# Attention on one core: K, Q and V loaded and outputs stored in groups of heads, waits folded into instructions

## Chip, cores, metric

One core of one Trainium2 chip. The metric is the device time of one execution in microseconds (us), from runs without a profile; the profile comes from a run of its own.

## The reference, cut to what matters

```python
B, H, Sq, Sk, D = 16, 32, 192, 1024, 128          # bfloat16
scores = jnp.einsum("bhqd,bhkd->bhqk", q, k) * D ** -0.5
p = softmax(scores, axis=-1)
out = jnp.einsum("bhqk,bhkd->bhqd", p, v)
```

There are 512 independent heads. Of each, the kernel reads 256 KB of K, 256 KB of V and 48 KB of Q, and writes 48 KB.

## The kernel before

All heads run through one software pipeline. A head has three units of 64 queries. A schedule of "virtual times" (one step is one unit) fixes each engine's order of instructions; semaphores do the rest. For each unit: QK on TensorE (8 matmuls), the maximum over key chunks on VectorE (`mx`), the maximum over partitions on GpSimd (`ar`), a bias matmul that subtracts it (`bi`), the exponential on ScalarE (`ex`). For each head: VectorE copies V beside a column of ones (`build_v`), TensorE multiplies P with it (`pv`), VectorE takes the reciprocal of the row sums (`rc`), ScalarE scales (`nm`), and the result is stored.

```python
NBK, NBQ, NBVR, NBV, NBO = 4, 3, 3, 2, 3      # slots: K, Q (4 heads each), V, V with ones, output
vt_lk = lambda h: NU * h - PFK * NU           # place of the K load in the order, PFK = 3 heads ahead
vt_lv = lambda h: vt_vc(h) - PFV * NU         # V: PFV = 2 heads ahead of its copy

def load_k(e, h=h, ks=ks):
    ins = e.dma_start_transpose(kT[:, ks], kf[h].rearrange("(kk c) d -> kk (c d)", c=NCH))
    if h >= NBK:
        ins.wait_op(s_qk, NU * (h - NBK + 1), "sem-ge")     # slot free
    ins.then_inc(s_k[ks], 16)

def load_v(e, h=h, vrs=vrs):
    ins = e.dma_start(vraw[:, vrs], vf[h].rearrange("(kk c) d -> kk c d", c=NCH))
    ...                                                     # same queue (SyncE) as K and Q

def build_v(e, h=h, vrs=vrs, vs=vs):
    if h >= NBV:
        e.wait_ge(s_pv, h - NBV + 1)                        # a wait of its own
    e.tensor_copy(v1[:, vs, :, 0:D], vraw[:, vrs]).wait_op(s_v[vrs], ...).then_inc(s_vc, 1)

def qk(e, ...):
    if j == 0:
        e.wait_ge(s_k[ks], 16 * (h // NBK + 1))             # a wait of its own
    ...
add("pe", vt_qk(u), qk)      # vt: u
add("dve", vt_mx(u), mx)     #     u + 1
add("pool", vt_ar(u), ar)    #     u + 2
add("pe", vt_bi(u), bi)      #     u + 3.4: after the QK of unit u + 3
```

## Time and profile before

| | us |
|---|---|
| median of 4 runs at first, of 16 in the end | 1340.7, 1342.2 |
| span of the profiled run | 1336.7 |
| TensorE's floor: 512 heads of 2.295 | 1175 |
| VectorE waiting for V | 131.0 |
| lost on TensorE before bias matmuls | 147 |

The last line is worked out from the trace: a bias matmul starts 29 ns after the last QK matmul if nothing is missing; what goes beyond is lost time of TensorE. (The page's idle time shows less of it, since the modelled ends of matmuls reach 160 ns over the next start.) The lines that carry this are in the prediction.

One more view: the loading queue (SyncE's) in order of time. Columns: start, length of the issue in us, queue, line, what.

```profile
646.02 1.17 SPq L153 DMA_TRANSPOSE qT<-in_q_dram  x1
647.24 1.31 SPq L146 DMA_TRANSPOSE kT<-in_k_dram  x1
648.59 0.58 SPq L160 DMA_DIRECT2D vraw<-in_v_dram  x1
649.21 1.24 SPq L146 DMA_TRANSPOSE kT<-in_k_dram  x1
650.50 0.74 SPq L160 DMA_DIRECT2D vraw<-in_v_dram  x1
651.28 1.46 SPq L146 DMA_TRANSPOSE kT<-in_k_dram  x1
652.79 0.57 SPq L160 DMA_DIRECT2D vraw<-in_v_dram  x1
653.40 1.34 SPq L146 DMA_TRANSPOSE kT<-in_k_dram  x1
654.79 0.57 SPq L160 DMA_DIRECT2D vraw<-in_v_dram  x1
```

Each issue starts 0.04 us after the last has ended. The queue is never idle: all its pauses over 0.1 us sum to 6 us of 1324.

### The profile page before, as it was taken

The numbers are of one execution on the slowest core, as the hardware profiler recorded it, in microseconds if no ns is written. First come the engines' busy times: TensorE is split into PE (matmuls) and PEld (weight loads), VectorE is DVE, ScalarE is ACT, GpSimd is POOL, SyncE is SP. The second block draws the span as 40 slices with busy tenths as digits, with TensorE's granted clock in tenths as the row PEclk, the third lists the DMA queues.
The fourth block names the chain that finished last, engine by engine and source line by source line (L and its number), as shares of the span: only waits on it lengthen the run. The fifth ranks groups of instructions, "written<-read, shape, count | busy, mean of one in ns | idle before, by whom it ended". The sixth has DMA issues, their size and how long they took to land.

```text
span 1336.7 us, 54938 instructions
## 1 busy us (share of the span) xinstructions
PE 1243.3 (93%) x22016; PEld 1049.0 (78%) x22016; DVE 1175.9 (88%) x2563; ACT 1115.3 (83%) x2561; POOL 861.3 (64%) x1540
## 2 busy tenths in 40 slices
PE   7999999999999999999999999999999999999997
PEld 6777788778887787878878787777887777877776
DVE  7888898899889898989888898888888898988886
ACT  6888888888888888888888888888888888888887
POOL 5666666666666666666666666666666666666665
PEclk9999999999999999999999999999999999999999
DMA  9999999999999999999999999999999999999998
GB/s 209 239 248 241 246 250 240 239 251 240 252 241 251 241 258 233 252 240 258 243 243 243 240 248 246 233 236 248 240 241 247 232 254 240 251 245 246 234 235 174
DMA packets 774397, 322.43 MB, mean 241 GB/s; under 512 B 659456, under 2 KB 708608, under 8 KB 774144
## 3 DMA queue, kind: packets, MB, share of 16 engines
q1 hardware_dynamic: 716800, 293.72, 107.9%
q10 hardware_dynamic: 57344, 25.20, 9.3%
q8 instruction: 176, 2.88, 0.9%
q14 instruction: 77, 0.63, 0.2%
HBM read 134.22 MB, written 25.17 MB: 119 GB/s over the span
## 4 chain that ended last, share of the span: by engine, by line
DMA 45%; PE 35%; DVE 9%; SPq 5%; POOL 4%; issue 2%; ACT 0%
DMA vraw<-in_v_dram 45%; PE ps L243 13%; PE ps L214 12%; PE ps L197 10%; DVE rmx L206 5%; SPq L146 5%; POOL hi L209 4%; DVE v L176 4%; DVE rinv L254 0%; SPq L153 0%; ACT osb L261 0%; ACT pT L222 0%
## 5 line engine op out<-in xcount | busy, mean ns | idle before, releaser
L209 POOL PARTITION_ALL_REDUCE hi<-rmx x1536 | 861.1, 561 | 469.8 <-DVE rmx L206 412.7
L206 DVE TENSOR_REDUCE rmx<-ps 128x64 bf16<-128x512 f32 x1536 | 986.1, 681 | 19.9 <-PE ps L197 6.9
L222 ACT ACTIVATE pT<-ps 128x512 bf16<-128x512 f32 x1536 | 853.8, 592 | 91.1 <-PE ps L214 57.7
L214 PE MATMUL ps<-hi,negsel 128*128 128x512 bf16 x1536 | 588.9, 383 | 84.6 <-POOL hi L209 81.3
L197 PEld LDWEIGHTS ps<-qT,kT 128*128 128x128 bf16 x12288 | 517.7, 98 | 128.0 <-issue 6.9
L197 PE MATMUL ps<-qT,kT 128*128 128x64 bf16 x12288 | 609.4, 193 | 5.9 <-DMA kT<-in_k_dram 5.8
L243 PEld LDWEIGHTS ps<-v,pT 128*96 128x96 bf16 x8192 | 550.2, 124 | 30.1
L243 PE MATMUL ps<-v,pT 128*96 128x129 bf16 x8192 | 568.4, 221 | 0.0
L261 ACT ACTIVATE osb<-ps,rinv 96x128 bf16<-96x128 f32 x1024 | 316.7, 358 | 127.6 <-DVE rinv L254 123.0
L176 DVE COPY v<-vraw 128x1024 bf16<-128x1024 bf16 x512 | 217.2, 424 | 134.7 <-DMA vraw<-in_v_dram 131.0
L214 PEld LDWEIGHTS ps<-hi,negsel 128*128 128x128 bf16 x1536 | 149.4, 97 | 126.5 <-POOL hi L209 104.0
L254 DVE RECIPROCAL rinv<-ps 96x2 f32<-96x2 f32 x512 | 79.4, 155 | 2.7 <-PE ps L243 2.7
L222 ACT ACT_TABLE_LOAD x1 | 1.3, 1283 | 0.7 <-PEq L309 0.7
L132 DVE MEMSET negsel<- 128x64 uint32 x1 | 0.1, 112 | 0.8 <-PEq L309 0.8
L309 POOL MEMSET const-float32-0.0<- 128x1 f32 x1 | 0.1, 98 | 0.2 <-issue 0.2
L133 DVE MEMSET negsel<- 1x128 bf16 x1 | 0.2, 165 | 0.1
L309 POOL MEMSET const-bfloat16-1.0<- 128x1 bf16 x1 | 0.1, 102 | 0.0
L309 POOL MEMSET const-uint8-127<- 128x1 uint8 x1 | 0.1, 101 | 0.0
L309 POOL MEMSET const-float32-1.0<- 128x1 f32 x1 | 0.1, 98 | 0.0
L134 DVE MEMSET v<- 128x16 bf16 x1 | 0.1, 72 | 0.0
## 6 DMA issues: line engine op xcount, KB each, us to landing
vraw<-in_v_dram SPq DMA_DIRECT2D x512, 256.0 KB, 4.4
out_dram<-osb ACTq DMA_DIRECT2D x512, 48.0 KB, 3.7
kT<-in_k_dram SPq DMA_TRANSPOSE x512, 4.9
qT<-in_q_dram SPq DMA_TRANSPOSE x128, 4.9
```

The source lines that it names most:

```text
L133: e.memset(negsel[0:1, :], -1.0).wait_op(s_init, 1, "sem-ge").then_inc(s_init, 1)
L146: ins = e.dma_start_transpose(kT[:, ks], kf[h].rearrange("(kk c) d -> kk (c d)", c=NCH))
L176: e.tensor_copy(v1[:, vs, :, 0:D], vraw[:, vrs]).wait_op(s_v[vrs], 16 * (h // NBVR + 1), "sem-ge").then_inc(s_vc, 1)
L197: ins = e.matmul(ps[:, bank, c * QW:(c + 1) * QW], kT[:, ks, c, :], rhs, start=(c == 0), stop=False, skip_group_check=True)
L206: e.tensor_reduce(rmx[:, rs, :], src, AX.X, ALU.max).wait_op(s_qk, u + 1, "sem-ge").then_inc(s_mx, 1)
L209: e.partition_all_reduce(hi[:, hs, :], rmx[:, rs, :], P, RMAX).wait_op(s_mx, u + 1, "sem-ge").then_inc(s_ar, 1)
L214: e.matmul(dst, negsel[:, :], rhs, start=False, stop=True, skip_group_check=True).wait_op(s_ar, u + 1, "sem-ge").then_inc(s_bi, 1)
L222: e.activation(pT[:, psl, :, q0:q0 + QW], src, ACTF.Exp, scale=scale).wait_op(s_bi, u + 1, "sem-ge").then_inc(s_ex, 1)
L243: ins = e.matmul(ps[0:MT, ob, t * (D + 1):(t + 1) * (D + 1)], lhsT, v1[:, vs, c, :], start=(c == 0), stop=(c == NCH - 1), skip_group_check ...
L254: e.reciprocal(rinv[0:MT, rvs, :].rearrange("p (t o) -> p t o", o=1), src).wait_op(s_pv, h + 1, "sem-ge").then_inc(s_rc, 1)
L261: ins = e.activation(osb[0:MT, osl, t, :], ps[0:MT, ob, t * (D + 1): t * (D + 1) + D], ACTF.Copy, scale=rinv[0:MT, rvs, t:t + 1])
L309: nc = _bacc.Bacc("TRN2", target_bir_lowering=False, num_devices=1)
```

## The change

Its intent: fewer and larger transfers (K in groups of 4 heads, Q of 8, V and stores of 2), issued earlier into more slots, and no separate wait instructions: a wait is hung on an earlier instruction that has none. With V loaded for two heads, the copy into `v1` takes two heads at once too.

```diff
-    GQ = cfg.get("GQ", 4)
-    NBK = cfg.get("NBK", 4)
-    NBQ = cfg.get("NBQ", 3)
+    GK = group(cfg.get("GK", 4))
+    GQ = group(cfg.get("GQ", 8))
+    GV = group(cfg.get("GV", 2))
+    GO = group(cfg.get("GO", 2))
+    NBK = cfg.get("NBK", 3)
+    NBQ = cfg.get("NBQ", 2)
     NBVR = cfg.get("NBVR", 3)          # slots are of groups now
-    PFK = cfg.get("PFK", 3)
-    PFV = cfg.get("PFV", 2)
+    PFK = cfg.get("PFK", 6.0)
+    PFV = cfg.get("PFV", 3.0)
 ...
+    def also_wait(self, sem, val, prod_vt, not_before=-1e30):
+        while self.free:                              # earlier instructions without a wait
+            ins, vt = self.free.pop()
+            if vt > prod_vt and vt >= not_before:
+                ins.wait_op(sem, val, GE)
+                return
+        self.free = []
+        self.eng.wait_ge(sem, val)
 ...
+                src = kf[gk * GK:(gk + 1) * GK].rearrange("g (kk c) d -> (g kk) (c d)", c=NCH)
+                dst = kT[:, slot].rearrange("p c g k -> p c (g k)")
+                ins = st.eng.dma_start_transpose(dst, src)
 ...
-                e.tensor_copy(v1[:, vs, :, 0:D], vraw[:, vrs])...
+                st.op(st.eng.tensor_copy(v1[:, slot, :, :, 0:D], src), vt_vc(gv), ...)   # GV heads
 ...
-                        e.wait_ge(s_k[ks], 16 * (h // NBK + 1))
+                        st.also_wait(s_k[ks], 16 * (gk // NBK + 1), vt_lk(gk))
```

## The prediction

> **What bounds the kernel now.** I read the page first, then the view of single source lines for the loads, then the timeline of VectorE and of TensorE over 608 to 614 us, a stretch that holds an undisturbed head (one of 512 attention heads) and a disturbed one.
>
> The page: the time to explain, the chain that ended last, and the one large wait for a transfer.
>
> ```profile
> span 1336.7 us, 54938 instructions
> ...
> DMA 45%; PE 35%; DVE 9%; SPq 5%; POOL 4%; issue 2%; ACT 0%
> ...
> L176 DVE COPY v<-vraw 128x1024 bf16<-128x1024 bf16 x512 | 217.2, 424 | 134.7 <-DMA vraw<-in_v_dram 131.0
> ```
>
> The chain runs through V loads for 45% of the span, and VectorE's copy of V is where it meets the engines: 131.0 us of waiting for V to land. No other wait for a transfer is over 6 us. The question is what a wait of VectorE is worth on TensorE. The timeline answers it (columns: start, length, engine, line, what it does; in brackets the idle time before). TensorE:
>
> ```profile
> 608.96 1.11 PE L243 MATMUL ps<-v,pT 128*96 128x129 bf16 x16
> 609.91 0.40 PE L197 MATMUL ps<-qT,kT 128*128 128x64 bf16 x8
> 610.14 0.38 PE L214 MATMUL ps<-hi,negsel 128*128 128x512 bf16 x1
> 610.36 0.40 PE L197 MATMUL ps<-qT,kT 128*128 128x64 bf16 x8
> ...
> 611.26 1.11 PE L243 MATMUL ps<-v,pT 128*96 128x129 bf16 x16
> ...
> 612.65 0.40 PE L197 MATMUL ps<-qT,kT 128*128 128x64 bf16 x8
> 613.20 0.39 PE L214 MATMUL ps<-hi,negsel 128*128 128x512 bf16 x1
> 613.42 0.40 PE L197 MATMUL ps<-qT,kT 128*128 128x64 bf16 x8
> 613.79 0.39 PE L214 MATMUL ps<-hi,negsel 128*128 128x512 bf16 x1
> ```
>
> Matmuls overlap, so read the distances between starts. Undisturbed, one head is: PV 0.95, then three times QK 0.23 and bias matmul (it subtracts the maximum) 0.215, which is 2.295 us, with no hole: 608.96 to 611.26. 512 x 2.295 = 1175 us is TensorE's floor. In the next head, the bias matmul comes 0.55 after its QK, then 0.37: 0.32 + 0.14 = 0.46 us lost. VectorE shows why:
>
> ```profile
> 608.66 0.16 DVE L254 RECIPROCAL rinv<-ps 96x2 f32<-96x2 f32 x1
> 608.74 0.41 DVE L176 COPY v<-vraw 128x1024 bf16<-128x1024 bf16 x1
> 609.06 1.98 DVE L206 TENSOR_REDUCE rmx<-ps 128x64 bf16<-128x512 f32 x3
> 610.96 0.16 DVE L254 RECIPROCAL rinv<-ps 96x2 f32<-96x2 f32 x1
> 611.37 0.56 DVE L176 COPY v<-vraw 128x1024 bf16<-128x1024 bf16 x1 [0.26 <-DMA vraw<-in_v_dram]
> 611.86 1.87 DVE L206 TENSOR_REDUCE rmx<-ps 128x64 bf16<-128x512 f32 x3
> ```
>
> From reciprocal to the next reduction is normally 0.40 us (0.08, then 0.32 for the copy). Here it is 0.90: V came late, and the copy took 0.49 instead of 0.32 of its engine. 0.50 late on VectorE became 0.46 on TensorE: the chain QK, maximum, copy, maximum, GpSimd all-reduce, bias matmul has almost no slack. Over the whole trace I compared the start times of every head: in the 48 heads whose reduction came 0.2 to 0.3 us late (mean 0.234) TensorE lost 0.169; where it came 0.02 late or less (246 heads) it lost 0.00. So the slack is about 0.06. Summed over all bias matmuls TensorE loses 147 us. With its first matmul at 5.8 us and 2.8 us after the last reciprocal: 5.8 + 1175 + 147 + 2.8 = 1331, which leaves 6 us for filling the pipeline.
>
> Why V is late: the view of the load lines gives counts and issue times (min/median/max ns).
>
> ```profile
> L146 SPq DMA_TRANSPOSE kT<-in_k_dram x512: 1237/1301/3208, 2.0 to 1320.2; - x171
> ...
> L160 SPq DMA_DIRECT2D vraw<-in_v_dram x512: 328/574/2532, 6.1 to 1324.9; - x171
> ```
>
> One queue issues all loads in order. At the smallest usual times a head costs it 1.24 (K) + 0.57 (V) + 1.17/4 (Q, one for four heads) + 2.25 x 0.045 between issues = 2.20 us, against 2.295 on TensorE. In addition each K load waits for a slot which is freed one 64-query unit before it is due, and V stands behind it. A V load takes 4.4 us to land and is due two heads (4.6 us) after its place in the order. Nothing can catch up.
>
> **What the Trainium skill says.** "Perfetto Trace Analysis", section "What 'DMA-bound' means", names the issuing sequencer as a bound of its own, when its track is solid with issues. The trace agrees: all issues of that queue together cover 1267 of 1337 us. "DMA: Bandwidth & Descriptors", section "Rules for kernel authors", advises coalescing and 1 MiB or more in a DMA; here V moves 256 KB each and lands in 4.4 us median. "Perfetto Trace Analysis", section "Optimizing Scalar/DVE Operations", puts VectorE's fixed cost on SBUF at about 60 ns for each instruction[...]. So of the copy's 0.32, some 0.26 grows with size. "Advanced Engine Details and Errata", section "VectorE Performance Modes", says that fast copies share a port with GpSimd and that the two hold each other up; the copy of 0.49 beside an all-reduce fits that.
>
> **The change part by part.**
> Loads: K for 4 heads (1 MB) in one issue, Q for 8, V for 2. Issues on the queue fall from 1152 to 448. If issue time grew in proportion to bytes, K and Q would cost what they do now (1.24 + 0.29 a head) and V at least no more, so about 2.0 us; if part is fixed, less. Buffers: K 3 x 4 heads, V 3 x 2 heads instead of 3. A K slot is now freed 7 units before the load's place in the order, not 1; a V slot comes free 6 heads before it is due, not 3. The transfer engines move the same 0.62 MB a head. The best 20 us of the trace ran at 279 GB/s, which is 2.23 us a head, and part of its loss lies between K and V transfers, of which there will be fewer. I take V's waits to go: up to 147 us off TensorE.
>
> VectorE: the copy now takes two heads at once, every second head. Total work falls (0.06 in two heads), but the order of instructions stays reciprocal, copy, three reductions, reciprocal, three reductions. So in every second head the copy takes 0.32 + 0.26 = 0.58 and the second reduction starts 0.26 late, exactly as if V had come 0.26 late. With 0.06 of slack TensorE loses 0.20 us in each pair. Nothing makes it good: VectorE idles 0.09 us before the next first reduction, since it waits for TensorE's QK. 256 x 0.20 = 51 us given back.
>
> Waits folded into instructions: the separate waits for V, output bank and K on TensorE's queue are gone, as are those on VectorE and ScalarE. TensorE shows no hole where they stand (608.96 to 609.91 is 16 matmuls at 59 ns with two such waits queued near it), so this is worth 0. The moved waits stand up to eight matmuls early; what they wait for is done some 1.5 us before.
>
> Stores: one for two heads; 0.32 us of ScalarE's queue saved in each pair, off the path: 0.
>
> Start: the first matmul needs 4 heads of K and 8 of Q. The first K loads land 1.2 us apart, so 5.8 + 3 x 1.2 + 0.7 = 10 us.
>
> Sum: 10 + 1175 + 51 + 2.8 + 6 = 1245 us; some V waits at the start and after Q loads, 6; the time without profile is some 3 us above the span (1340.7 against 1336.7, 1338.6 against 1336.7). **1254 us.**
>
> **Rivals.**
> Bursts: V now stands behind 1 MB of K and every other time 384 KB of Q. Issue at today's rate is 5.2 + 2.4 + 0.6, then 4 to 6 us to land: 12 to 14 us, against 6 heads x 2.4 = 14.4 between a slot's release and its use. It fits barely. If the 64 Q-bearing groups miss by 1 us each, the time is near 1320; that VectorE's wait is today spread over 184 heads, rather than concentrated where Q is loaded, speaks against it.
> No pinch: the larger copy is absorbed, and TensorE runs at its floor: 1254 - 51 = 1203. The late heads above speak against it.
> A worse pinch: the longer copy meets an all-reduce each time and is held 0.17 longer, as at 611.37: 256 x 0.17 = 44, so 1298. Undisturbed copies at 0.32 meet one too, at the same place in the order, so I doubt it.
> Waits that cost after all: two semaphore instructions of 51 ns a head on TensorE's queue would be 52 us if they were exposed, and the time 1203.
>
> **Range and chances.** The floor cases end near 1203, the bad ones at 1298 to 1320. Most weight lies on the pinch: 8 in 10 for 1212 to 1295. Faster by over 2% means under 1314; only large remaining bursts miss that: 0.92, within 2% 0.07, slower 0.01.
>
> **What the changed profile would show.** Right: VectorE's wait for V under 30 us; 256 copies of about 0.67 us each, their successor starting 0.58 after them; TensorE's PV starts alternating by 2.3 and 2.5 us (4.8 a pair), with the bias matmuls after a copy late by 0.2 together; issues covering well under 1000 us. Wrong: even spacing of 2.3 (no pinch), large waits for V in every second K group (bursts), or the issue time of a 1 MB K load far over 5 us.

## The result, and the profile after

The changed kernel takes 1262.2 us (median of 11, 1259.7 to 1266.7), against 1342.2 before (16 runs). The ratio is 0.9396, with a 95% interval of 0.9373 to 0.9420. Ratios here are the mean time of one kernel's fast runs over that of the other's in the same rounds, so not quite the ratio of the medians. The forecast was 1254, with a range of 1212 to 1295.

The page of the changed kernel: span, chain of waits by engine, the bias matmul's group and the copy's (busy us, mean ns of one | idle before).

```profile
span 1259.0 us, 51172 instructions
...
PE 94%; DMA 3%; DVE 1%; SPq 1%; POOL 0%; issue 0%; ACT 0%; POOLq 0%
...
L260 PE MATMUL ps<-hi,negsel 128*128 128x512 bf16 x1536 | 589.8, 384 | 5.6 <-POOL hi L254 5.3
...
L207 DVE COPY v<-vraw 128x2048 bf16<-128x2048 bf16 x256 | 172.6, 674 | 4.8 <-DMA vraw<-in_v_dram 4.5
```

The wait for V has gone from 131.0 to 4.5 us, and the chain now runs through TensorE. But a chain that is 94% TensorE isn't yet TensorE at its floor. Its timeline, after:

```profile
603.15 1.11 PE L289 MATMUL ps<-v,pT 128*96 128x129 bf16 x16
604.09 0.40 PE L238 MATMUL ps<-qT,kT 128*128 128x64 bf16 x8
604.33 0.38 PE L260 MATMUL ps<-hi,negsel 128*128 128x512 bf16 x1
604.54 0.40 PE L238 MATMUL ps<-qT,kT 128*128 128x64 bf16 x8
604.86 0.39 PE L260 MATMUL ps<-hi,negsel 128*128 128x512 bf16 x1
605.09 0.40 PE L238 MATMUL ps<-qT,kT 128*128 128x64 bf16 x8
605.46 0.39 PE L260 MATMUL ps<-hi,negsel 128*128 128x512 bf16 x1
605.68 1.11 PE L289 MATMUL ps<-v,pT 128*96 128x129 bf16 x16
```

From PV to PV this head takes 2.53 us, not 2.295. The first bias matmul comes 0.24 after its QK, the second 0.32, the third 0.37: 0.23 us lost. VectorE at the same time:

```profile
602.24 0.69 DVE L250 TENSOR_REDUCE rmx<-ps 128x64 bf16<-128x512 f32 x1 [0.42 <-PE ps L238]
602.84 0.15 DVE L300 RECIPROCAL rinv<-ps 96x2 f32<-96x2 f32 x1
602.92 0.67 DVE L207 COPY v<-vraw 128x2048 bf16<-128x2048 bf16 x1
603.51 1.88 DVE L250 TENSOR_REDUCE rmx<-ps 128x64 bf16<-128x512 f32 x3
605.30 0.16 DVE L300 RECIPROCAL rinv<-ps 96x2 f32<-96x2 f32 x1
605.38 1.26 DVE L250 TENSOR_REDUCE rmx<-ps 128x64 bf16<-128x512 f32 x2
```

The copy of two heads occupies 0.59 us (602.92 to 603.51) where one head took 0.32, and the reductions behind it are late by the difference. Then VectorE idles 0.42 us in the next head: it has time enough in two heads, but not at the place where the copy stands. This repeats: over the trace the PV starts lie 2.29 and 2.535 us apart in turn (medians), 4.83 a pair.

The loading queue, after:

```profile
633.49 6.76 SPq L171 DMA_TRANSPOSE kT<-in_k_dram  x1
640.30 1.14 SPq L194 DMA_DIRECT2D vraw<-in_v_dram  x2
641.88 6.36 SPq L171 DMA_TRANSPOSE kT<-in_k_dram  x1
648.28 1.09 SPq L194 DMA_DIRECT2D vraw<-in_v_dram  x2
651.53 1.37 SPq L182 DMA_TRANSPOSE qT<-in_q_dram  x1
652.95 6.44 SPq L171 DMA_TRANSPOSE kT<-in_k_dram  x1
```

It now pauses (649.37 to 651.53: the slot of Q is not free yet); pauses over 0.1 us sum to 132 us. The loads have overtaken TensorE. What doesn't fit the forecast: a K load for four heads takes 6.4 us to issue, more than four single ones (4 x 1.24).

### The profile page after: what moved, and what is told of

Read it like the earlier page. It is cut to its first block, busy times and chain, and to the rows that moved or that the text cites. A ratio compares the mean times of both kernels' runs of the same rounds, so it can differ in the third digit from the quotient of the medians.

```text
span 1259.0 us, 51172 instructions
## 1 busy us (share of the span) xinstructions
PE 1240.7 (99%) x22016; PEld 1035.8 (82%) x22016; DVE 1130.5 (90%) x2307; ACT 1116.0 (89%) x2561; POOL 912.7 (72%) x1540
## 4 chain that ended last, share of the span: by engine, by line
PE 94%; DMA 3%; DVE 1%; SPq 1%; POOL 0%; issue 0%; ACT 0%; POOLq 0%
PE ps L289 37%; PE ps L260 30%; PE ps L238 27%; DMA vraw<-in_v_dram 3%; SPq L171 1%; DVE rmx L250 1%; DVE v L207 1%; POOL hi L254 0%; SPq L182 0%; ACT osb L309 0%; POOLq L119 0%; DVE rinv L300 0%
## 5 line engine op out<-in xcount | busy, mean ns | idle before, releaser
L254 POOL PARTITION_ALL_REDUCE hi<-rmx x1536 | 912.5, 594 | 340.7 <-DVE rmx L250 247.7
L207 DVE COPY v<-vraw 128x2048 bf16<-128x2048 bf16 x256 | 172.6, 674 | 4.8 <-DMA vraw<-in_v_dram 4.5
```

The costliest lines, as they stand in the source:

```text
L207: st.op(st.eng.tensor_copy(v1[:, slot, :, :, 0:D], src), vt_vc(gv), wait=(s_v[rslot], 16 * (gv // NBVR + 1))).then_inc(s_vc, 1)
L254: st.op(st.eng.partition_all_reduce(hi[:, hs, :], rmx[:, rs, :], P, RMAX), vt_ar(u), wait=(s_mx, u + 1)).then_inc(s_ar, 1)
```

## The experiments

The theory at the outset: (1) V came late since its queue was full and had no lead (a load's head start on its use); the change cures that; (2) the doubled copy then holds TensorE up by 0.2 us a pair, here called the pinch; (3) folded waits are worth nothing. Rivals: batching itself raises the rate of the transfers; the pinch only keeps time with some other bound; folded waits are what helps. Each kernel was timed beside the kernel before on the same chip (4 runs of it, 7 of before).

| run | what | median us | ratio to before | queue: us a head / pauses, us | VectorE waits for V, us |
|---|---|---|---|---|---|
| before | | 1342.2 | 1 | 2.59 / 6 | 131.0 |
| after | the change | 1262.2 | 0.9396 | 2.42 / 132 | 4.5 |
| e1 | after, single copies | 1256.3 | 0.9336 | 2.41 / 27 | 55.6 |
| e2 | folded waits alone | 1354.9 | 1.0074 | 2.62 / 7 | 147.4 |
| e3 | slots and lead, no groups | 1362.7 | 1.0121 | 2.62 / 3 | 155.9 |
| e4 | groups, two slots | 1293.7 | 0.9621 | 2.50 / 375 | 36.6 |
| e7 | e1, half of V | 1197.6 | 0.8918 | 2.30 / 284 | 3.4 |
| e8 | after, half of V | 1258.5 | 0.9370 | 2.41 / 350 | 3.2 |
| e9 | e1, V from ScalarE's queue | 1588.6 | 1.1795 | 3.04 / 76 | 278.7 |
| e10 | K in fours alone | 1356.4 | 1.0089 | 2.60 / 207 | 3.2 |
| e11 | e1 with twice the slots | 1253.3 | 0.9336 | 2.40 / 1 | 55.0 |
| e12 | e10 with more slots | 1280.5 | 0.9531 | 2.46 / 2 | 78.7 |
| e13 | V and stores in twos, K single | 1377.6 | 1.0267 | 2.66 / 2 | 169.5 |
| e14 | e11 with groups twice as large | 1246.6 | 0.9272 | 2.37 / 1 | 7.4 |

"Us a head" is the time from the first issue of the loading queue to the end of its last, over 512; "pauses" is the sum of its gaps over 0.1 us. A queue with no pauses shows what the load path can do; one with pauses waits for slots, so something else is the bound. In e9 the queue carries K and Q alone. In e14 K comes late too: TensorE waits 30 us for it. In all tables and diffs a slot holds one group. e7 and e8 give a wrong result; all others were correct.

### e1: one copy for each head

```diff
-            def build_v(st, gv=gv):                     # 2 heads
-                st.op(st.eng.tensor_copy(v1[:, slot, :, :, 0:D], src), ...)
+            for iv in range(GV):                        # 1 head, at its own place
+                def build_v(st, gv=gv, iv=iv):
+                    st.op(st.eng.tensor_copy(v1[:, slot, iv, :, 0:D], src), vt_vch(h), ...)
```

> The changed kernel, but VectorE copies V one head at a time (loads still two heads at a time). Theory 1, the pinch: the doubled copy delays the second reduction by 0.27 us and TensorE loses 0.22 us in every pair of heads, about 57 us in all; with single copies that goes, and the time is 1200 to 1210. Rival: the spacing of 2.29 and 2.54 has another cause (loads, folded waits, the extra waits for V), and then the time stays within 10 us of 1262.

Measured: 1256.3, the rival's range. The spacing of undisturbed heads did go to 2.29 (the median), but another wait has taken the place of the pinch. The waits of e1 (engine, line, waited for: us in total, times, longest):

```profile
DVE v L210 <- DMA vraw<-in_v_dram: 55.6, 59, 2.9
```

59 waits of 0.9 us on average, about one for each Q load. The pinch was gone and the time hardly moved: either the pinch was never the bound, or a second bound stands just behind it. e7 and e8 tell these apart.

### e2: folded waits alone

```diff
-    GK = group(cfg.get("GK", 4))        # likewise GQ 8 -> 4, GV 2 -> 1, GO 2 -> 1,
+    GK = group(cfg.get("GK", 1))        # NBK 4, NBQ 3, NBVR 3, PFK 3, PFV 2: as before the change
```

> Only the waits are folded into instructions; group sizes, buffers and order places are those of the kernel before. Theory 1, folded waits are worth nothing since TensorE shows no hole where they stood: 1335 to 1347. Rival: two semaphore instructions a head of 51 ns on TensorE's queue were exposed: up to 52 us less, 1290 to 1310.

Measured: 1354.9, ratio 1.0074 (1.0024 to 1.0124): no gain, a small loss, and outside both ranges. The waits name a line which the kernel before doesn't have among its waits:

```profile
ACT osb L309 <- DMA out_dram<-osb: 55.9, 86, 1.9
```

The wait for a free output slot now hangs on an instruction without a wait, and on ScalarE the nearest is the second scaling of the previous head. So the slot is asked for one head too early, and three slots serve as two. With two heads in a store (six heads of slots) the wait doesn't occur in the changed kernel.

### e3: slots and lead without groups

```diff
-    GK 4, GQ 8, GV 2, GO 2, NBK 3, NBQ 2, NBVR 3          # defaults, PFK 6 and PFV 3 are kept
+    GK 1, GQ 4, GV 1, GO 1, NBK 12, NBQ 3, NBVR 6
```

> No grouping at all (1152 issues, as before), but the buffers and order places of the changed kernel in heads: K 12 heads, V 6 heads, loads placed 6 and 3 heads ahead. Theory 1, the lead of the loads did it, not their size: the issues cost 2.20 us a head against TensorE's 2.295, so the queue just keeps up and V waits nearly vanish; copies are of one head, so there is no pinch either: 1200 to 1230. Rival, the number of issues did it: the queue stays nearly full, V stays late, 1300 to 1345.

Measured: 1362.7, the rival's side of it, even slower than expected; 11 us of the loss against before are e2's (folded waits and the output slot; 41.6 us of that wait here). The first half of my theory falls: with slots for 12 heads of K the queue never waits for one, has no pauses, and still moves a head in 2.62 us. Lead is worthless when the path itself is too slow: what a queue without pauses needs for a head, 2.62 us, is more than TensorE's 2.295.

### e4: groups with less lead

```diff
-    NBK = cfg.get("NBK", 3); NBVR = cfg.get("NBVR", 3); PFK 6.0; PFV 3.0
+    NBK = cfg.get("NBK", 2); NBVR = cfg.get("NBVR", 2); PFK 4.0; PFV 2.0
```

> The groups of the changed kernel, but two slots for K and V in place of three, and K placed 4 heads ahead, V 2 heads ahead. Theory 1, the lead did it: V stands behind a K load whose issue takes 6.4 us and lands 5.6 us after its own issue, more than the 4 heads (9.6 us) of its slots allow, so V waits come back at every K load: 1300 to 1400. Rival, the larger transfers did it: 1260 to 1280.

Measured: 1293.7, between the two. V waits come back (36.6 us), but 50 us of the gain remain. So with large groups the third slot and the earlier place in the order (both were taken away) are worth about 31 us; the rest of the gain the groups give even without them.

### e7 and e8: the same, with half of V's bytes

```diff
+                if gv < NBVR:       # first groups whole; later ones stale in the second half
+                    ins = st.eng.dma_start(vraw[:, slot], src)
+                else:
+                    HW = NCH * D // 2
+                    ins = st.eng.dma_start(vraw[:, slot, :, 0:HW], src[:, :, 0:HW])
```

> Single copies as in e1, and after the first groups each V load moves only half of its bytes (wrong result on purpose; as many issues as in e1). Theory 2, formed after e1 and e3: the load path itself has a limit near 2.40 us a head, which e1 ran into when the pinch was gone; with a fifth of the bytes gone TensorE reaches its floor of 2.295 a head: 1195 to 1210. Rival, e1 is held by something that is not the amount of data (the pinch theory is wrong, folded waits, VectorE): 1245 to 1260.

> The changed kernel with half V loads in the same way (wrong result on purpose), copies of two heads. Theory 1, the pinch is a bound of its own: 4.83 us a pair stays, 1250 to 1262. Rival, the changed kernel is held by the load path and the pinch only keeps time with it: under 1230.

Measured: 1197.6 with single copies and 1258.5 with copies of two heads. Both are what the pinch theory says. In both the queue pauses for some 300 us, so loads don't matter. Span and chain of e7, then of e8:

```profile
span 1195.6 us, 51428 instructions
...
PE 76%; DVE 22%; SPq 1%; DMA 0%; issue 0%; POOL 0%; POOLq 0%; ACT 0%
```

```profile
span 1257.2 us, 51172 instructions
...
PE 98%; SPq 1%; DMA 0%; DVE 0%; POOL 0%; ACT 0%; issue 0%; POOLq 0%
```

The difference, 61 us, is the cost of copying two heads at once. In e8 the bias matmuls lose 62 us, in e7 4 us. This also settles e1: there the load path, at 2.40 us a head, stood just behind the pinch, at 4.83 / 2 = 2.415. The change has two bounds within 1%, so that taking away either one shows almost nothing (e1: 6 us, e8: 4 us) and both together 65.

### e9: V from another queue

```diff
-    LV_ENG = cfg.get("LV_ENG", "sp")
+    LV_ENG = cfg.get("LV_ENG", "act")      # on e1
```

> e1 with the V loads issued from ScalarE's queue. Theory 2a, the limit of the load path is in the issuing queue: it loses 0.29 us of issue a head, and the time falls to 1200 to 1225. Theory 2b, the limit is in the transfers (the issue is only held back by them): the same bytes and transfers, 1240 to 1265, and K waits appear on TensorE.

Measured: 1588.6, far outside both. The transfers became slower. The page's line of packets, in e1 and in e9:

```profile
DMA packets 751845, 322.11 MB, mean 257 GB/s; under 512 B 636928, under 2 KB 686080, under 8 KB 751616
```

```profile
DMA packets 751845, 322.11 MB, mean 203 GB/s; under 512 B 636928, under 2 KB 686080, under 8 KB 751616
```

The same packets took longer: in the median a K load took 10.0 us to issue (7.1 in e1) and 16.2 to land (10.8), and V 10.0 us to land (5.6). So taking V's issues off the queue gained nothing here: the transposes and the plain transfers of the second queue both became slower. The run doesn't say how. Not all of the 332 us need be theirs: V's issues now also wait their turn among ScalarE's instructions, and TensorE's granted clock was 0.929 (0.997 in e1) and its busy time 1297 us (1199).

### e10, e12, e13: which of the groups

```diff
 e10:  GK 4, NBK 3 kept;  GQ 4, NBQ 3, GV 1, NBVR 6, GO 1 (NBO 3)
 e12:  e10 with  NBQ 4, NBVR 8, NBO 8, PFV 4
 e13:  GK 1, NBK 12;  GQ 4, NBQ 4, GV 2 (single copies), NBVR 6, GO 2, NBO 6, PFV 4
```

> K in groups of four, all else single as in e3 (Q 4, V 1, stores 1), with deep buffers. Per-transfer theory: from e3 to e1 the transfers fall from 3.25 to 1.25 a head and the spacing from 2.62 to 2.40, 0.11 us each; grouping K takes away 0.75 of them, so 1320 or a little under, 1300 to 1330. Switching theory: what costs is each change between a transpose and plain transfers; K in fours makes them as few as in e1, so 1250 to 1275.

Measured: 1356.4, worse than both. Not for loads: V waits 3.2 us, and the queue pauses 207 us. The single stores now run beside loads of 1 MB, they take up to 8.0 us to land (6.3 in e3), and three output slots, which serve as two (e2), don't cover that:

```profile
ACT osb L309 <- DMA out_dram<-osb: 183.9, 161, 3.8
```

So the run decides nothing about the load path, and e12 repeats it with enough slots.

> e10 with eight slots for stores and for V (e10 was held by its three store slots behind the long K transfers). If grouping K alone frees the load path, 1200 to 1260; if what costs is the number of transfers (2.5 a head here, 3.25 in e3, 1.25 in e1), 1300 to 1330.

Measured: 1280.5, in the middle between the two ranges, so neither theory has it. Against e3 82 us are gained. The store waits that e3 still has (up to 32 us of TensorE's losses) need not be taken off: neither queue pauses, and its step from 2.62 to 2.46 us a head makes 82 us by itself, 0.21 for each of the 384 K transposes saved.

> The opposite: K single (12 slots), Q in fours, V in twos (copied singly) and stores in twos, with deep slots. If grouping K is what frees the load path, this stays at 1320 to 1362 as e3; if the number of transfers counts (2.25 a head here), 1280 to 1320.

Measured: 1377.6, above both ranges, and 15 us above e3. With K single, larger groups of V and of stores gain nothing at all. The view of the K line shows it from the queue's side (count: issue time min/median/max in ns), e13, then e11, where K is in fours and all else alike but Q, in eights, and the slots:

```profile
L172 SPq DMA_TRANSPOSE kT<-in_k_dram x512: 1231/1838/4487, 2.0 to 1358.7; - x171
```

```profile
L172 SPq DMA_TRANSPOSE kT<-in_k_dram x128: 4227/7078/8469, 2.1 to 1217.8; - x128
```

From e13 to e11 the queue goes from 2.66 to 2.40 us a head, 1378 to 1253 us, with 384 fewer K transposes and 64 fewer of Q: some 0.28 us for each, if they share it evenly. With e12 that gives an estimate of 0.2 to 0.3. Issue times themselves don't get smaller: they are as long as the transfers hold them up. e7 shows that too: its issues cover 881 us where the same ones of e1 cover 1190; only the bytes differ.

### e11: more slots

```diff
-    NBK 3, NBQ 2, NBVR 3, NBO 3, PFK 6, PFV 3        # e1
+    NBK 6, NBQ 4, NBVR 8, NBO 6, PFK 12, PFV 9
```

> e1 with about twice the slots (K 6 groups, Q 4, V 8, stores 6), so that the load queue is stopped neither by a slot nor by bursts. Theory A, grouped loads can keep up with TensorE and e1 was held by the Q slots and the burst after them: V waits nearly vanish, 1200 to 1220. Theory B, the grouped load path moves a head in no less than 2.40 us however deep the buffers: 1245 to 1260, the queue never idle.

Measured: 1253.3, Theory B. The queue of e11 has no pause (1 us in all), TensorE still loses 61 us to late V:

```profile
639.54 6.83 SPq L172 DMA_TRANSPOSE kT<-in_k_dram  x1
646.41 1.13 SPq L195 DMA_DIRECT2D vraw<-in_v_dram  x2
647.58 3.26 SPq L183 DMA_TRANSPOSE qT<-in_q_dram  x1
650.89 7.18 SPq L172 DMA_TRANSPOSE kT<-in_k_dram  x1
```

So 2.40 us a head is what the load path gives with these groups, however deep the buffers. The burst after each Q load, which e1 seemed to show, is only where the lack comes to light.

### e14: larger groups

```diff
-    GK 4, NBK 6, GV 2, NBVR 8, GO 2, PFV 9           # e11
+    GK 8, NBK 3, GV 4, NBVR 6, GO 4, PFV 12          # copies still single
```

> e11 with groups twice as large: K 8 heads, V 4 (copied singly), stores 4, Q 8; slots for 24 heads. If each K transfer costs a fixed 0.21 us (e3 to e12: 82 us for 384 fewer) and each other one 0.047 (e12 to e11: 27 us for 576 fewer, with Q), 64 fewer K and 256 fewer others save 13 + 12 = 25 us of e11's 1253, and the first matmul comes some 4 us later: 1225 to 1240. Rival, at groups of four the bytes alone set the pace: 1250 to 1262.

Measured: 1246.6, between the ranges: the queue takes 2.37 us a head, and the first matmul starts at 12.6 us (9.4 in e11). The gain of larger groups is running out. By its median it is the fastest correct kernel here, 0.9272 of before (0.9231 to 0.9314), where the change has 0.9396; the interval of e11 (0.9290 to 0.9383) overlaps with it.

## Why the prediction was right, and where not

- *Bound before.* That TensorE loses 147 us because V is late, and that V is late because one queue is full, held. The reasons given for the full queue did not. The forecast took the smallest issue times (2.20 us a head) for what the queue costs; it really took 2.59, because issues are held up by the transfers. And "in addition each K load waits for a slot" plays no part: with twelve slots (e3) nothing is gained.
- *V's waits go.* They did: 4.5 us are left, within the 6 allowed. "Loads" and "Buffers" were credited together; e3, e12 and e13 show that K in groups does most of it (2.62 to 2.46 us a head, then 2.40 with the others), and e4 that slots and lead are needed on top for about 31 us.
- *The copy of two heads.* The step was right in kind, place and nearly in size: 0.27 us later (forecast 0.26), 0.04 of it absorbed (forecast 0.06); forecast 0.20 lost a pair, measured 0.224 (means of the two bias matmuls after an undisturbed copy, 0.086 and 0.138). Over 256 pairs 57 us, forecast 51. By e7 and e8 61. The fixed part behind the forecast, about 60 ns by the Trainium skill ("Perfetto Trace Analysis", section "Optimizing Scalar/DVE Operations"), agrees with the copies: 0.32 us for one head and 0.59 for two leave 0.05.
- *Folded waits.* Forecast 0. In the changed kernel nothing speaks against it; but no run takes them out of it, so there their worth of 0 is not shown; alone they cost 0.7% (e2), and the waits point to the output slot, asked for a head too early.
- *The sum.* 10 for the first matmul (9.6), 1175, 51 (57, and 6 more of bias waits, mostly at the start), 2.8 (3.0), 6 (7.5 lost at other matmuls), 6 for V: 1251 in the profile, and 1259 was measured. The pinch's size is most of the error of 8 us.
- *The signs to look for.* PV in turn 2.3 and 2.5, copies of 0.67, V waits under 30: right. Issues "covering well under 1000 us": wrong, 1090. A K issue "far over 5 us" was named as a sign of bursts: it is 6.4, and the changed kernel shows no bursts of V waits.
- *The rivals.* "No pinch: TensorE at its floor, 1203" was wrong twice over: even without the pinch the load path would have held the kernel at 1253 to 1256. The forecast counted on the best 20 us of the trace (2.23 us a head) as a rate that can be kept; the rate that can be kept is 2.40. That the number came out right is partly luck: the pinch, which was seen, hides by 1% a limit that was not. "A worse pinch" (1298) didn't come: the reduction after a copy starts 0.59 us after it in the median, as forecast, and not 0.17 later.

What stays open is why a transpose for one head costs the path 0.2 to 0.3 us more than its share of a larger one. The packets in the traces say where the time sits, but not why: half of the packets of transposes take 18 ns or less, and those over 0.2 us add up, shared over 16 engines, to 0.65 us a head in e3, 0.47 in e12 and 0.43 in e11, while those up to 60 ns take 1.37 to 1.40 in all three. So in these runs the difference goes with a few slow packets, and not with the rate of the others (packets overlap in time, so these are shares and no sum). Alternation between transposes and plain transfers isn't enough of a reason: e13 has half as many changes between K and V as e3 and is no faster.

## What to carry to other kernels

Before crediting a batch of transfers with saved issues or deeper buffers, run one kernel with the buffers alone and look whether the queue still has no pauses: then its rate is the bound, and only what changes the rate helps. When a per-item instruction on a second engine is made twice as long and half as frequent, its average falls but its longest delay doubles; in a chain without slack the delay is what counts. And if taking away a bound shows nothing, take away the suspected second one with it (here by moving half the bytes) before dropping the theory.

## What the Trainium skill lacked or had wrong

- "Advanced Engine Details and Errata", section "X-Bar Transpose (TRN2)", says that transposing DMAs are as fast as regular ones, and expects 350 to 400 GB/s, some 90% of a plain copy. Here they weren't: inside a 1 MB K load of the changed kernel about 282 packets of 256 B end in each 0.25 us (289 GB/s), in V loads at their best about 48 of 2048 B (393 GB/s); both counted from the trace's packets.
- "DMA: Bandwidth & Descriptors", section "DMA Transpose (X-bar)", gives no fixed cost of a transpose. Here K by single heads against K by fours made 2.62 against 2.46 us a head (e3, e12), and 2.66 against 2.40 with Q in larger groups too (e13, e11): an estimate of 0.2 to 0.3 us for each transpose saved. Grouping the plain transfers alone gave nothing (e3 1362.7, e13 1377.6).
- The same page, section "Issuing engines are not separate DMA queues", says that issuing from several engines only saves issue time. It can cost a lot beside transposes: V from ScalarE's queue took the kernel from 1256 to 1589 us, and a K load then took 16.2 us to land, not 10.8 (e1, e9).
- "Perfetto Trace Analysis", section "What 'DMA-bound' means", takes a solid issuing track for descriptor generation. Here the track is solid because transfers hold the issues up: the same issues cover 1190 us in e1 and 881 in e7, where V moves half the bytes. A solid track alone doesn't tell which of the two is the bound.
